# Scores of 256 queries in one go in five PSUM banks, with q and k turned in fp32 ahead of their split: thresholded attention and a MoE layer on one core

## The chip, the cores and the metric

The kernel runs on one core of one Trainium2 chip. The metric is device time in microseconds (us) from the first to the last instruction of the program; the median of three runs before the change is 545.32 us. Engines are called as in the profile: PE is TensorE (PEld its weight loads), DVE is VectorE, ACT is ScalarE, POOL is GpSimd, and SP is SyncE, which here issues most DMAs.

## What is computed

```python
# batch 8, heads 8, seq 576, head_dim 64; tau 0.02
scores = q @ k.T / sqrt(64)                        # per batch and head, 576 x 576
scores = where(scores >= max(scores) - tau, scores, -1e9)
attn   = exp(scores - max(scores)); attn /= sum(attn) + 1e-9
x      = (attn @ v), heads side by side            # 4608 tokens x 512
out    = leaky_relu(x @ w_in, 0.01) @ w_out        # 512 -> 2048 -> 512
```

q, k, v, the weights and the output are fp32 in DRAM. The threshold lies only 0.02 below the maximum, so the scores must be near fp32: q and k are each multiplied by 64 and split into two fp16 halves (high and low), and three products (high x high, low x high, high x low) are summed in PSUM.

## The kernel before

Each batch has 576 queries: two blocks of 256 and a tail of 64. Heads go in pairs; the first head of a pair has rows 0 to 63 of every turned tile, the second rows 64 to 127. A **step** is 128 queries of a head pair (`c` is the half of the 256-query block): `scores` (L195) runs twelve matmuls of 288 columns into two PSUM tiles of two banks each, which are double buffered; `copy_min` (L213) scales and copies them to SBUF on DVE with a running minimum (the scores are negated); `threshold` (L222) adds tau on POOL; `exps` (L226) and `weights` (L254) make the thresholded weights, on ACT and DVE, or, for one of the two heads of a "steep" step, on ACT alone (L242 and L243). After two steps, `recip` (L260) on DVE and `widen` (L264) on POOL put the reciprocal sums beside the weights, and `turn_w` (L268) has SP issue a transposing DMA of the weights. Four steps later `pv` (L273) multiplies by v, and `evacuate` (L287) scales the result into `x` on DVE. There are 18 steps in a batch, 144 in all: 64 of the pairs are full ones, 16 steps are tails of two head pairs each.

When four pairs of a block have their `x`, sixteen MoE units are queued: `layer1` (L315) multiplies by w_in into PSUM tile `hp` and applies the leaky ReLU on ACT (`g`), `layer2` (L331) accumulates `g` times w_out into PSUM tile `o`, which ACT copies to `osb`; `store` (L346) writes it out. In each step one `layer1` and two `layer2` calls are issued.

q and k of the next batch are loaded by SP (L73, L82), multiplied by 64 and split on POOL (L128, L139, L144) into fp16 halves, and each half is turned by PE (`turn`, L160: eight fp16 transposes for a unit, which is one head pair of q or k) into a PSUM tile that shares the tag "h" and its two buffers with `hp`; ACT copies the turned halves to `qT` and `kT` (L181). PSUM's eight banks go to scores (4), "h" (2), `pv` (1) and `o` (1).

The schedule is manual: every engine works in the order in which the loop at L454 issues, and each instruction waits on semaphores. The tables `loads_at`, `turns_at` and `pool_at` say in which step loads, turns and splits are issued. SP's queue holds the loads, the transposing DMAs and the stores, in the order of issue.

Of the kernel before, what the change touches and what calls it, by code (L numbers as in the profile page):

```python
# [14 lines left out]
PV_LAG = 4  # L15
# [12 lines left out]
class Step:  # L28


    def __init__(self, n, b, blk, p, c):
        self.n, self.b, self.blk, self.p, self.c = n, b, blk, p, c
        self.tail = blk == 2
# [3 lines left out]
def kernel(  # L37
# [24 lines left out]
    ident = sb.tile([128, 128], FP16, name="ident")  # L62
    minus_tau = sb.tile([128, 1], FP32, name="minus_tau")


# [3 lines left out]

    raws, tails, vraws, vtails = {}, {}, {}, {}  # L70
    SRC = {"q": q, "k": k}

    def load_main(b, s, which, eng=None, parts=1):  # L73
        t = sb.tile([128, 4, 256], FP32, tag="raw", bufs=4, name="raw")
        n = 4 // parts
        for i in range(parts):
            (eng or nc.sync).dma_start(
                out=t[:, ds(n * i, n), :],
                in_=SRC[which][b, ds(4 * s + n * i, n), 0:MAIN, :].rearrange("h (p t) d -> p h (t d)", t=4))
        raws[b, s, which] = t  # L80

    def load_tails(b, which, eng=None):  # L82
        t = sb.tile([128, 2, 2, 64], FP32, tag="rawt", bufs=2, name="rawt")
        src = SRC[which][b, :, MAIN:S, :].rearrange("(u sh) p d -> u p sh d", u=2)
        for u in range(2):
            (eng or nc.sync).dma_start(out=t[ds(64 * u, 64), :, :, :].rearrange("p s h d -> p (s h) d"), in_=src[u])
        tails[b, which] = t
# [23 lines left out]

    WIDE = {"q": 576, "k": 640}
    turned, halves, scaled = {}, {}, {}
# [6 lines left out]
    def pair_of(b, p, which):  # L122
        return raws[b, p // 2, which][:, ds(2 * (p % 2), 2), :].rearrange("p h (t d) -> p h t d", d=64)

    def new_half():
        return sb.tile([128, 2, 4, 2, 64], FP16, tag="half", bufs=4, name="half")

    def split_scale(key):  # L128
        t = sb.tile([128, 4, 2, 64], FP32, tag="scaled", bufs=2, name="scaled")
        if key[1] == "t":  # L130
            src = tails[key[0], key[2]][:, :, :, :]
            dst = t[:, 0:2, :, :]
        else:
            src = pair_of(*key)
            dst = t[:, :, :, :].rearrange("p t h d -> p h t d")
        nc.gpsimd.tensor_scalar(out=dst, in0=src, scalar1=64.0, scalar2=1.0, op0=AX.mult, op1=AX.mult)  # L136
        scaled[key] = t

    def split_high(key):  # L139
        n = 2 if key[1] == "t" else 4  # L140
        halves[key] = new_half()
        nc.gpsimd.tensor_copy(out=halves[key][:, 0, 0:n, :, :], in_=scaled[key][:, 0:n, :, :])  # L142

    def split_low(key):  # L144
        n = 2 if key[1] == "t" else 4
        nc.gpsimd.tensor_tensor(out=halves[key][:, 1, 0:n, :, :], in0=scaled.pop(key)[:, 0:n, :, :],  # L146
                                in1=halves[key][:, 0, 0:n, :, :], op=AX.subtract)

    def split_now(key):
        t = halves[key] = new_half()  # L150
        for i in range(2):
            if key[1] == "t":
                src, n = tails[key[0], key[2]][:, :, i, :], 2
            else:
                src, n = pair_of(*key)[:, i, :, :], 4
            nc.scalar.activation(out=t[:, 0, 0:n, i, :], in_=src, func=AF.Copy, bias=0.0, scale=64.0)  # L156
            nc.vector.scalar_tensor_tensor(out=t[:, 1, 0:n, i, :], in0=src, scalar=64.0, in1=t[:, 0, 0:n, i, :],
                                           op0=AX.mult, op1=AX.subtract)

    def turn(key, copy=None):  # L160
        copy = copy or nc.scalar.copy
        b, p, which = key
        dst, half = turned_of(b, which), halves.pop(key)
        n = 2 if p == "t" else 4
        c0 = 0 if which == "q" else 64
        if p == "t":
            c0 = MAIN if which == "q" else 0
            tp = ps.tile([128, 2, 2, 2, 64], FP16, tag="h", bufs=2, name="tp")
        else:
            tp = ps.tile([128, 2, 4, 128], FP16, tag="h", bufs=2, name="tp")  # L170
        for x in range(2):
            for t in range(n):
                o = tp[:, x, :, t, :] if p == "t" else tp[:, x, t, :]
                nc.tensor.transpose(o, half[:, x, t, :, :].rearrange("p h d -> p (h d)"), ident[:, :])  # L174
        if p == "t":
            for x in range(2):
                copy(out=dst[:, x, :, ds(c0, 64)], in_=tp[:, x, :, :, :].rearrange("d u s p -> d (u s) p"))
            if which == "k":
                nc.gpsimd.tensor_copy(out=dst[:, :, :, 576:640], in_=dst[:, :, :, 0:64])
        else:  # L180
            copy(out=dst[:, :, p, ds(c0, 512)], in_=tp[:, :, :, :].rearrange("d x t p -> d x (t p)"))  # L181

    steps = []
    for b in range(B):
        for blk in range(2):
            for p in range(NP):
                for c in range(2):
                    steps.append(Step(len(steps), b, blk, p, c))  # L190
        for c in range(2):
            steps.append(Step(len(steps), b, 2, 2 * c, c))
    PERB = len(steps) // B

    def scores(st):  # L195
        st.sc = [ps.tile([128, 2, 512], FP32, tag="sc", bufs=2, name=f"sc{h}") for h in range(2)]
        for kh in range(2):
            for i, (qx, kx) in enumerate(((0, 0), (1, 0), (0, 1))):
                for u in range(2 if st.tail else 1):
                    for h in range(2):  # L200
                        pair = st.p + u
                        rows = ds(64 * h, 64)
                        key0 = 64 * (1 - h) + 288 * kh
                        if st.tail:
                            lhs = turned[st.b, "q"][rows, qx, pair, MAIN:S]
                            o = st.sc[h][ds(64 * u, 64), kh, 0:288]
                        else:
                            lhs = turned[st.b, "q"][rows, qx, pair, ds(256 * st.blk + 128 * st.c, 128)]
                            o = st.sc[h][:, kh, 0:288]
                        nc.tensor.matmul(out=o, lhsT=lhs, rhs=turned[st.b, "k"][rows, kx, pair, ds(key0, 288)],  # L210
                                         start=(i == 0), stop=(i == 2), skip_group_check=True)

    def copy_min(st):  # L213

        st.mn = sb.tile([128, 2], FP32, tag="mn", bufs=3, name="mn")
        st.s = sb.tile([128, 2, 576], FP32, tag="s", bufs=2, name="s")
        for h in range(2):
            nc.vector.tensor_scalar(  # L218
                out=st.s[:, h, :].rearrange("p (a b) -> p a b", a=2), in0=st.sc[h][:, :, 0:288],
                scalar1=-1.0 / UNIT, scalar2=None, op0=AX.mult, op1=AX.min, accum_out=st.mn[:, h : h + 1])  # L220

    def threshold(st):  # L222
        st.th = sb.tile([128, 2], FP32, tag="th", bufs=3, name="th")
        nc.gpsimd.tensor_scalar(out=st.th[:, :], in0=st.mn[:, :], scalar1=1.0, scalar2=tau_f, op0=AX.mult, op1=AX.add)  # L224

    def exps(st):  # L226

        c = 0 if st.tail else st.c
        if c == 0:
            pairs["now"] = pr = Pair()  # L230
            pr.w = sb.tile([128, 2, 10, 128], FP16, tag="w", bufs=3, name="w")
            pr.sum = sb.tile([128, 2, 2], FP32, tag="sum", bufs=3, name="sum")
            pr.n = 1 if st.tail else 2
        st.pair = pr = pairs["now"]
        flat = pr.w[:, c, :, :].rearrange("q n d -> q (n d)")
        st.w = [flat[:, ds(576 * h, 576)] for h in range(2)]
        st.sum = [pr.sum[:, c, h : h + 1] for h in range(2)]
        st.e = sb.tile([128, 2, 576], FP16, tag="e", bufs=2, name="e")
        for h in range(2):
            if h and st.steep:  # L240
                z = st.s[:, h, :]
                nc.scalar.activation(out=z, in_=z, func=AF.Prelu, bias=st.th[:, h : h + 1], scale=-1.0, alpha=1e20)  # L242
                nc.scalar.activation(out=st.w[h], in_=z, func=AF.Exp, bias=minus_tau[:, :], scale=1.0,  # L243
                                     accum_out=st.sum[h])
            else:
                nc.scalar.activation(out=st.e[:, h, :], in_=st.s[:, h, :], func=AF.Exp, bias=st.mn[:, h : h + 1],  # L246
                                     scale=-1.0)

    pairs = {}

    class Pair:
        pass
# [267 lines left out]
```

## Time and profile before

| | |
|---|---|
| runs, us | 541.51, 545.32, 548.29; median 545.32 |
| profiled execution: span, us | 545.5 |
| its mean granted TensorE clock | 0.967 |
| first and last score matmul, us from the start | 8.1 and 503.3 |
| first layer 1 matmul | 63.1 |
| last weights on DVE | 508.0 |
| full transposing DMAs on SP: number, median time of the issue | 68, 3.25 us |
| DMA moved | 90.04 MB, 165 GB/s |

The span is the profiled execution's own time, from its first to its last instruction. Busy time counts an engine's instructions and not its waits; idle time ahead of a group is put down to the instruction that ended it. For SP the rows are issues: a DMA's row ends when its descriptors are handed over, and landing comes later (5.2 us in the median from issue to landing for the transposing DMAs). The chain of waits is followed back from the last instruction.

### The profile page before, as it was taken

To read this page: it belongs to the slowest core of one execution; us is meant where nothing else is said; L and a number is where in the kernel's file an instruction comes from. 1 tells how busy PE (TensorE), PEld (TensorE's weight loads), DVE (VectorE), ACT (ScalarE), POOL (GpSimd) and SP (SyncE) were. 2 spreads that over 40 slices of the span, in tenths; PEclk is the share of its full clock that TensorE was granted. 3 is DMA by queue.
4 is the path that set the end of the run, shared out by engine and by line. 5 is a ranking of instruction groups with operands and counts; after the bars stand their busy time and mean duration, and the time that the engine had idled before them with its cause. 6 is when DMAs were issued, how large, how long until landed. Compare 5 with 4: busy or idle time off the path is not lost.

```text
span 545.5 us, 14102 instructions
## 1 busy us (share of the span) xinstructions
PE 495.6 (91%) x5312; PEld 315.6 (58%) x5312; DVE 422.5 (77%) x1163; ACT 428.2 (79%) x726; POOL 319.8 (59%) x562
## 2 busy tenths in 40 slices
PE   4557656799999999999999999999999999999996
PEld 2334434565665666666666666666666666656672
DVE  3458555889899998899889988999889988788200
ACT  3678645687888888898889888898888888999541
POOL 5777553967676667767676767666676764112000
PEclk9987678899999999999999999999999999999999
DMA  9868999557997789698978899798988876767601
GB/s 211 226 162 151 200 155 170 119 116 154 216 211 143 169 196 193 166 193 154 219 150 190 150 210 195 163 192 185 203 164 169 169 171 144 144 110 136 136 40 58
DMA packets 231044, 90.04 MB, mean 165 GB/s; under 512 B 201280, under 2 KB 227904, under 8 KB 230976
## 3 DMA queue, kind: packets, MB, share of 16 engines
q1 hardware_dynamic: 227744, 84.43, 76.2%
q0 software_dynamic: 2688, 4.19, 5.1%
q8 instruction: 41, 0.67, 0.5%
q10 hardware_dynamic: 544, 0.52, 0.3%
q14 instruction: 27, 0.22, 0.1%
HBM read 36.70 MB, written 9.44 MB: 85 GB/s over the span
## 4 chain that ended last, share of the span: by engine, by line
PE 70%; DVE 10%; DMA 8%; POOL 4%; issue 4%; ACT 3%; SPq 0%; POOLq 0%; DVEq 0%
PE hp L324 21%; PE o L336 20%; PE sc L210 18%; PE pv L282 8%; DMA wT<-w 6%; DVE s L218 5%; DVE w L256 4%; PE tp L174 4%; DMA raw<-in_k_dram 2%; POOL half L142 1%; POOL scaled L136 1%; POOL half L146 1%; ACT w L243 1%; DVE x L304 1%; ACT s L242 1%
## 5 line engine op out<-in xcount | busy, mean ns | idle before, releaser
L218 DVE TENSOR_SCALAR_CACHE_REDUCE s<-sc 128x576 f32<-128x576 f32 x288 | 204.8, 749 | 70.3 <-PE sc L210 62.8
L256 DVE SCALAR_TENSOR_TENSOR w<-s,th,e 128x576 f16<-128x576 f32 x210 | 190.7, 930 | 2.4 <-POOL th L224 1.7
L210 PE MATMUL sc<-kT,qT 64*128 64x288 f16 (+1 forms) x1920 | 146.4, 299 | 17.8 <-DVE s L218 10.2
L246 ACT ACTIVATE e<-s,mn 128x576 f16<-128x576 f32 x210 | 155.8, 774 | 5.1 <-DVE s L218 5.1
L336 PE MATMUL o<-wout,g 128*128 128x512 f16 x576 | 146.8, 379 | 0.7 <-ACT osb L342 0.7
L324 PE MATMUL hp<-x,win 128*128 128x256 f16 x1024 | 136.7, 277 | 0.2 <-ACT g L326 0.2
L324 PEld LDWEIGHTS <-win 128*128 128x128 f16 x1280 | 106.1, 99 | 44.3 <-issue 31.9
L210 PEld LDWEIGHTS <-qT 64*128 64x128 f16 (+1 forms) x1920 | 81.2, 100 | 77.2 <-issue 52.3
L265 POOL CAST w<-rec 128x256 f16<-128x256 f32 (+1 forms) x80 | 30.1, 376 | 149.5 <-DVE rec L262 138.5
L326 ACT ACTIVATE g<-hp 128x512 f16<-128x512 f32 x144 | 84.2, 585 | 40.0 <-PE hp L324 39.1
L242 ACT ACTIVATE s<-s,th 128x576 f32<-128x576 f32 x78 | 60.4, 774 | 53.9 <-POOL th L224 53.6
L146 POOL TENSOR_TENSOR half<-scaled,half 128x512 f16<-128x512 f32 (+1 forms) x77 | 83.0, 1079 | 6.0
L336 PEld LDWEIGHTS <-g 128*128 128x128 f16 x576 | 53.4, 98 | 38.3 <-issue 1.2
L282 PE MATMUL pv<-wT,v 128*64 128x256 f16 (+1 forms) x960 | 57.4, 257 | 19.9 <-DMA wT<-w 14.5
L282 PEld LDWEIGHTS <-v 128*64 128x64 f16 x960 | 37.4, 112 | 52.9 <-issue 23.8
L142 POOL CAST half<-scaled 128x512 f16<-128x512 f32 (+1 forms) x77 | 61.9, 804 | 4.9
L243 ACT ACTIVATE w<-s,minus_tau 128x576 f16<-128x576 f32 x78 | 60.5, 775 | 2.5
L174 PE MATMUL tp<-ident,half 128*128 128x128 f16 x576 | 49.0, 231 | 6.6 <-ACT half L156 5.0
L136 POOL TENSOR_SCALAR scaled<-raw 128x512 f32<-128x512 f32 x62 | 49.4, 796 | 4.8 <-DMA raw<-in_k_dram 1.4
L224 POOL TENSOR_SCALAR th<-mn 128x2 f32<-128x2 f32 x144 | 40.8, 283 | 17.1 <-DVE s L218 4.5
L174 PEld LDWEIGHTS <-half 128*128 128x128 f16 x576 | 40.7, 104 | 12.1 <-ACT half L156 5.0
L181 ACT COPY kT<-tp 128x1024 f16<-128x1024 f16 x32 | 32.1, 1004 | 0.0
(32 smaller groups left out, 245.2 us busy)
## 6 DMA issues: line engine op xcount, KB each, us to landing
vraw<-in_v_dram SPq DMA_DIRECT2D x16, 512.0 KB, 5.1
out_dram<-osb SPq DMA_DIRECT2D x16, 512.0 KB, 3.4
raw<-in_k_dram SPq DMA_DIRECT2D x14, 512.0 KB, 4.3
raw<-in_q_dram SPq DMA_DIRECT2D x14, 512.0 KB, 4.7
win<-in_moe_w_in_dram POOLq DMA_DIRECT2D x4, 512.0 KB, 9.9
wout<-in_moe_w_out_dram POOLq DMA_DIRECT2D x4, 512.0 KB, 12.1
wT<-w SPq DMA_TRANSPOSE x80, 5.2
raw<-in_k_dram SPq DMA_DIRECT2D x4, 256.0 KB, 10.6
```

The costliest lines, as they stand in the source:

```text
L142: nc.gpsimd.tensor_copy(out=halves[key][:, 0, 0:n, :, :], in_=scaled[key][:, 0:n, :, :])
L146: nc.gpsimd.tensor_tensor(out=halves[key][:, 1, 0:n, :, :], in0=scaled.pop(key)[:, 0:n, :, :], in1=halves[key][:, 0, 0:n, :, :], op=AX.sub ...
L174: nc.tensor.transpose(o, half[:, x, t, :, :].rearrange("p h d -> p (h d)"), ident[:, :])
L210: nc.tensor.matmul(out=o, lhsT=lhs, rhs=turned[st.b, "k"][rows, kx, pair, ds(key0, 288)], start=(i == 0), stop=(i == 2), skip_group_check= ...
L218: nc.vector.tensor_scalar(out=st.s[:, h, :].rearrange("p (a b) -> p a b", a=2), in0=st.sc[h][:, :, 0:288], scalar1=-1.0 / UNIT, scalar2=No ...
L243: nc.scalar.activation(out=st.w[h], in_=z, func=AF.Exp, bias=minus_tau[:, :], scale=1.0, accum_out=st.sum[h])
L246: nc.scalar.activation(out=st.e[:, h, :], in_=st.s[:, h, :], func=AF.Exp, bias=st.mn[:, h : h + 1], scale=-1.0)
L256: nc.vector.scalar_tensor_tensor(out=st.w[h], in0=st.s[:, h, :], scalar=st.th[:, h : h + 1], in1=st.e[:, h, :], op0=AX.is_le, op1=AX.mult, ...
L282: nc.tensor.matmul(out=o, lhsT=v16[st.b % 2][:, st.p + u, blk, :], rhs=rhs, start=(i == 0), stop=(i == 4), skip_group_check=True)
L324: nc.tensor.matmul(out=hp[:, jj, :], lhsT=w_in16[:, i, ts(j, 128)], rhs=g.x[:, i, :], start=(i == 0), stop=(i == 3), skip_group_check=True)
L326: nc.scalar.activation(out=g.g[:, ds(nj * u, nj), :], in_=hp[:, :, :], func=AF.Prelu, bias=0.0, scale=1.0, alpha=0.01)
L336: nc.tensor.matmul(out=g.o[:, :], lhsT=g.g[:, j, ts(m, 128)], rhs=w_out16[:, j, :], start=(j == 0), stop=(j == 15), skip_group_check=True)
```

## The change

The loop's unit becomes a **period**: 256 queries of a head pair (four score tiles of 128 x 576), or the tails of all four pairs; 9 in a batch, 72 in all. Each period issues two rounds of MoE (a round is one `layer1` and two `layer2`), so as many rounds per query as before. The scores of a period lie in one PSUM tile of five banks, `sc`, which is not double buffered. The four tiles of 576 columns stand side by side and cross bank borders, so each is computed in two pieces; pieces of both heads share bank 2, and a dependency is added by hand that keeps the second head's piece there (`b12`) behind the first head's (`a12`). It goes over SP: a `nop` on SP waits for the matmul of `a12`, and the matmul of `b12` waits for the `nop`.

The threshold of a period becomes one DVE instruction for its four tiles, three tiles go the plain way (exp on ACT, weights on DVE) and one the steep way (ACT alone), always. One transposing DMA per period takes the weights out; pv follows two periods later, and its PSUM tile moves to tag "h". q and k are turned in fp32: POOL multiplies and reorders a unit (`bring`), PE turns it with four fp32 transposes, ACT takes it out as fp32 (`take_out`), and POOL then splits it into the halves (`split`). The three units turned ahead of the loop are split by ACT and DVE straight from PSUM, and batch 0 is loaded head by head with the order of elements that the turn needs, so it isn't brought.

Order of issue in period n: loads and stores (SP), scores, four copies and threshold, turns and take-outs, POOL's splits and brings, then exp, MoE round, two exps, MoE round, steep pair, pv of period n-2, two weights, `x` of period n-2, the third weights, reciprocal, widening and transpose.

```diff
-PV_LAG = 4
+PV_LAG = 2
...
+    sc = ps.tile([128, 2560], FP32, name="sc")
+    PLACE = {(0, 0): 128, (1, 0): 704, (0, 1): 1856, (1, 1): 1280}
...
+    def scores(st):
+        (a00, a01), (b01, b00) = pieces(0, 0), pieces(0, 1)
+        (a11, a12), (b12, b11) = pieces(1, 0), pieces(1, 1)
+        todo = [[(1, a12), (0, a00), (0, a01), (1, a11)], [(0, b00), (0, b01), (1, b11), (1, b12)]]
...
+            for mm in product(st, c, h, x, i):
+                if (h, x) == (1, b12) and i == 0:
+                    tc.add_manual_dep(mm.ins, signal.ins.name, BEHIND, reason="the row halves share a bank")
+                last = mm
+            if (h, x) == (0, a12) and i == 2:
+                signal = nc.sync.nop()
+                tc.add_manual_dep(signal.ins, last.ins.name, BEHIND, reason="the row halves share a bank")
...
+    def copies(st):
...
+        for n, t in enumerate(TILES):
+            st.s[t] = sb.tile([128, 576], FP32, tag=f"s{n}", bufs=1, name="s")
+            nc.vector.tensor_scalar(out=st.s[t][:, :], in0=sc[:, ds(PLACE[t], 576)], scalar1=-1.0 / UNIT, scalar2=None,
+                                    op0=AX.mult, op1=AX.min, accum_out=st.mn[:, n : n + 1])
+        nc.vector.tensor_scalar(out=st.th[:, :], in0=st.mn[:, :], scalar1=1.0, scalar2=tau_f, op0=AX.mult, op1=AX.add)
...
+    def finish(st):
+        rec = sb.tile([128, 2, 2], FP32, tag="rec", bufs=2, name="rec")
+        nc.vector.reciprocal(out=rec[:, :, :], in_=st.sum[:, :, :])
+        nc.gpsimd.tensor_copy(out=st.w[:, :, 9, :].rearrange("q c (h d) -> q c h d", h=2),
+                              in_=rec[:, :, :].unsqueeze(3).to_broadcast([128, 2, 2, 64]))
+        st.wt = sb.tile([128, 2, 10, 128], FP16, tag="wT", bufs=4, name="wT")
+        nc.sync.dma_start_transpose(out=st.wt[:, :, :, :].rearrange("k c n q -> k (c n) q"),
+                                    in_=st.w[:, :, :, :].rearrange("q c n d -> q (c n d)"))
...
-        st.pv = ps.tile([128, 4, 128], FP32, tag="pv", bufs=1, name="pv")
+        st.pv = ps.tile([128, 2, 128], FP32, tag="h", bufs=2, name="pv")
...
+            tp = ps.tile([128, 4, 128], FP32, tag="h", bufs=2, name="tp")
+            src = ready.pop(key)
+            for t in range(4):
+                nc.tensor.transpose(tp[:, t, :], src[:, t, :, :].rearrange("p h d -> p (h d)"), ident[:, :])
...
+        for h in range(2):
+            eng.dma_start(out=t[:, :, h, :], in_=SRC[which][0, 2 * p + h, 0:MAIN, :].rearrange("(p t) d -> p t d", t=4))
...
+        while stores:
+            store()
+        st = periods[n] if n < N else None
+        if st:
+            scores(st)
+            copies(st)
+        for key in turns_at.get(n, []):
+            turn(key)
+            take_out(key)
```

## The prediction

> **What bounds the kernel now.** I read the page first: busy shares, then the slices of clock, then the chain that ended last.
>
> ```profile
> PE 495.6 (91%) x5312; PEld 315.6 (58%) x5312; DVE 422.5 (77%) x1163; ACT 428.2 (79%) x726; POOL 319.8 (59%) x562
> PEclk9987678899999999999999999999999999999999
> PE 70%; DVE 10%; DMA 8%; POOL 4%; issue 4%; ACT 3%; SPq 0%; POOLq 0%; DVEq 0%
> PE hp L324 21%; PE o L336 20%; PE sc L210 18%; PE pv L282 8%; DMA wT<-w 6%; DVE s L218 5%; DVE w L256 4%; PE tp L174 4%; DMA raw<-in_k_dram 2%; POOL half L142 1%; POOL scaled L136 1%; POOL half L146 1%; ACT w L243 1%; DVE x L304 1%; ACT s L242 1%
> ```
>
> The reader is to see that TensorE is the bound from about 110 us on, and that SP (SPq) has no share: nothing on the chain waits for SP's queue. Next I read the grouped rows for the price of one instruction, and the timeline for pitches and for SP.
>
> ```profile
> L218 DVE TENSOR_SCALAR_CACHE_REDUCE s<-sc 128x576 f32<-128x576 f32 x288 | 204.8, 749 | 70.3 <-PE sc L210 62.8 <-ACT g L326 1.7 <-ACT osb L342 1.4
> L265 POOL CAST w<-rec 128x256 f16<-128x256 f32 x64 | 25.5, 398 | 125.9 <-DVE rec L262 115.0 <-POOL v L110 5.7 <-issue 4.2
> L262 DVE RECIPROCAL rec<-sum 128x4 f32<-128x4 f32 x64 | 11.4, 178 | 5.5 <-ACT w L243 0.9
> ```
>
> ```profile
> 297.31 3.01 SPq L270 DMA_TRANSPOSE wT<-w  x1
> ...
> 300.38 0.58 SPq L77 DMA_DIRECT2D raw<-in_q_dram  x1
> ...
> 302.90 0.18 DVE L262 RECIPROCAL rec<-sum 128x4 f32<-128x4 f32 x1
> ...
> 303.14 0.40 POOL L265 CAST w<-rec 128x256 f16<-128x256 f32 x1 [1.27 <-DVE rec L262]
> 303.57 3.88 SPq L270 DMA_TRANSPOSE wT<-w  x1
> ```
>
> Two things to see: the transpose starts 0.03 us after the widening that it needs (303.54), so its row holds no wait for it; and SP's next instruction (300.38) starts only when the transpose's 3.01 us are over. Issuing one transpose holds SP's queue for 3 to 4 us (68 full ones: median 3.25). Last, the clock beside TensorE's work:
>
> ```profile
> 72.05:75.46 3.41, 0.00 (x0) 0.00 (x0) 2.51 (x6) 1.62 (x3) 3.35 (x5) 1.00 1.33 181
> 75.46:78.87 3.41, 1.42 (x14) 0.91 (x18) 0.00 (x0) 1.65 (x3) 2.98 (x6) 0.50 1.45 145
> 78.87:82.29 3.42, 3.42 (x36) 1.95 (x32) 1.94 (x6) 0.12 (x1) 0.16 (x1) 0.50 1.09 101
> 82.29:89.11 6.82, 2.21 (x40) 1.68 (x32) 4.16 (x12) 4.63 (x7) 5.06 (x9) 1.00 1.34 129
> ```
>
> Columns: window, PE, PEld, DVE, ACT, POOL busy, granted clock, DMA. A window of 3.41 us with an idle PE is followed by half clock, until a window full of work has passed.
>
> **The change, part by part.** Pitches (start to next start, medians of the steady timeline): score block of 12 matmuls 0.84, of layer 1 0.88, of layer 2 (four matmuls) 0.96, pv 0.67, eight fp16 transposes 0.45; copy 0.68, weights 0.74 to 0.81, plain exp 0.67, Prelu of `hp` 0.48, the steep pair 0.80 + 0.87. The steady pace now: scores start at 8.1 and end at 503.3 us, 72 pairs of steps, about 6.84 us each, of which PE has 2 x (0.84 + 0.88 + 0.96) + 0.67 + 1.11 x 0.45 = 6.5.
>
> What the change lightens: take-outs of 512 fp32 values (as `g` from `hp`, pitch 0.48) for copies of 1004 ns, 64 of them, some 25 us of ACT; 144 thresholds (283 ns, 40.8 us) leave POOL for 72 small DVE instructions, 0.15 each by the reciprocal of the same shape; 80 transposing DMAs become 72. None of this is on PE, so alone it is worth little. Summed per period, DVE would have 5.9, ACT 5.4 us. Matmul columns of scores, layers and pv are unchanged.
>
> PE's fp32 transposes: four per unit instead of eight. No row shows an fp32 transpose. Lower end 56 ns each as fp16, 0.22 a unit; upper end four times that, 0.90 (1.11 units a period). I take the lower; the upper adds 0.55 to a period in the loop below. The Trainium skill ("FP8 and Floating Point Precision", TensorE Precision Notes) says that true fp32 takes four passes through the array; by it the sum would stand at the upper end. No run here shows it yet.
>
> The new wait. In each period the first of the last three matmuls of head 1 (`b12`) waits for a signal that SP passes on (`nc.sync.nop`). SP works in order, and what stands ahead of signal n in its queue is: the transpose of period n-1, which waits for POOL's widening, which waits for the reciprocal that ends DVE's work on period n-1; then the loads and stores of period n. Behind `b12` on PE stand the turns, both rounds of layers 1 and 2, and pv of period n. And `sc` is one tile, so the first copy of period n waits for the last score matmul. DVE issues the copies of period n after the reciprocal of n-1, and pv, exp and weights of period n come before the reciprocal of n. So the wait closes a ring over SP that is passed once per period. Its length from reciprocal to reciprocal, at full clock, in us:
>
> - Reciprocal's end to widening 0.07, widening 0.40, to SP 0.03, issue of the transpose 3.25: 3.74. Two of the 68 issues took over 8 us, early in the run; I take the median, and 3.05 and 3.53 (the mean) as ends.
> - SP's loads and stores: 15.5 of them in nine periods at 0.58 to 0.70 with 0.04 between: 1.12 a period. Signal at 4.94.
> - SP to PE, bounded by 0.03 to 0.1 like other handoffs, 0.07; weights 0.1, three matmuls of 256 columns 0.32, drain 0.17: copies start at 5.63 and end, with the read of the last minimum, at 8.42; threshold done 8.65.
> - PE goes on at 5.43: turn to 5.66, first `hp` 6.64, second 8.5, pv ready 10.1.
> - ACT in order: take-out 5.9, exp 6.5, Prelu 7.2, two exps from 7.65, Prelu 9.0, half an `osb` 0.24, steep pair 9.7 to 11.4.
> - DVE: weights 8.65 and 9.4, `x` 10.2, third weights 10.55 to 11.4, reciprocal done 11.6.
>
> A period of 11.6 us against 6.84, and TensorE stands idle for about 5.2 of it (scores up to `b12` of the next period are done by 11.4, the signal comes at 4.94 of the next). By the rows on the clock, an idle stretch of 5.2 us leaves at least one 3.41 us window mostly empty, so the work after the signal starts at half clock, for 2.6 to 5.8 us depending on where the windows fall. Every microsecond at half clock puts the second `hp` and pv half a microsecond later, and both are on the way to the reciprocal: 1.3 to 2.9 us more, 12.9 to 14.5. A period longer than four windows moves the next window's boundary nearer to the signal, and the half-clock stretch shrinks with it; a shorter one does the opposite. So the period is drawn to four windows, 4 x 3.413 = 13.65 us. I take this value; the upper price of fp32 transposes changes the stretch, not the four windows.
>
> Start and end. SP's first loads become 20 issues for 16, in runs of 256 bytes, and each beyond the eighth waits for an earlier landing; now SP is through at 19.5 us, I take 22 (19 to 27) for the first signal and 5.3 from copies to reciprocal: 28. Five periods without MoE at 11.2 (10.9 at full clock): 56. 66 periods x 13.65 = 901. After the last reciprocal eleven iterations of MoE remain, 32.5 on PE, and 5 until the store has landed; 38, as now 37.5 from the last weights (508.0) to the end. Sum: 28 + 56 + 901 + 38 = 1023 us. The profiled span, 545.5, agrees with the median of the runs, 545.32, so nothing is added.
>
> Edits at nothing: POOL's split (0.8 + 1.1 a unit, plus 0.8 to bring) lies in the long period beside the ring; without that cover it would delay the widening, which stands behind it on POOL. pv in the `h` buffers: its third user; the buffer it takes was freed by a Prelu a microsecond earlier.
>
> **The rivals.**
> 1. The ring as above, with the clock kept (a partly busy window need not count as idle: 82.29 to 89.11 kept full clock over two windows with 2.21 us of work, the second of them empty): 28 + 5 x 10.9 + 66 x 11.6 + 38 = 886. The upper fp32 price makes it 922.
> 2. Other side: the signal does not wait behind the transpose. Then PE's own 6.0 + 0.6 per period decides: 10.6 + 72 x 6.6 + 38 = 524, faster by 4%. Against it stands every SP row: the next instruction never starts within a transpose's span. It decides only if the signal comes within 0.2 us of the reciprocal, since without the relay the ring is 6.7.
> 3. SP's share is short. The Trainium skill ("DMA: Bandwidth & Descriptors", Issuing engines are not separate DMA queues) says that the time to initiate a DMA on a sequencer is usually small relative to the DMA itself. As a mechanism of this kernel: the transpose is issued like a load, 0.58 for 3.25, the ring is 8.95, and the time 28 + 5 x 8.3 + 66 x 8.95 + 38 = 698. The rows say 3.0 to 3.9 of 5.2 us to landing.
>
> **How the numbers follow.** The ring with half clock 0.57, with full clock 0.30, short issue 0.04, no ring 0.09. About 2% is what a measurement of this kernel tells from no change. Only the last case holds faster (0.05) and same (0.04); slower has 0.91. The predicted time is that of the first case, 1023 us. Its own ends: 12.9 to 15 us a period, 973 to 1112; the second case's lower end, with an issue of 3.05, is 873. The range 870 to 1110 takes in both and leaves out some 2 in 10.
>
> **What would show it.** Right: in the profile after, PE's weight loads of scores or SPq among the waits, with idle PE of over 4 us in every period; SPq rows of the transpose followed at once by the signal, then by the last score matmuls, then by four copies in a row; DVE's idle time ahead of the copies some 5 us x 72; granted clock of 7 in the steady slices, against 9 for rival 1; DMA_TRANSPOSE still about 3.2 on SP. The fp32 transposes' pitch settles their price. Wrong: a period under 8 us, or a PE busy above 80% at full clock, would mean that the signal is not held up by the transpose.

## The result, and the profile after

The changed kernel takes 1045.69 us (median of four runs, 1043.32 to 1047.84), the kernel before 546.4 beside it (541.51 to 548.29): 1.916 times as long, 95% interval 1.905 to 1.926. It is slower by far more than a measurement can miss. The profiled execution has a span of 1044.5 us at a mean granted clock of 0.776. (Runs of the kernel before scatter from 536 to 553 us over all that follows, and the ratios are made from undisturbed runs alone, so a ratio is not always the quotient of the two medians beside it.)

The page of the changed kernel: busy time, PE's and the clock's slices, the chain, and four groups with the idle time ahead of them.

```profile
PE 641.1 (61%) x5024; PEld 403.3 (39%) x5024; DVE 477.1 (46%) x1227; ACT 404.0 (39%) x693; POOL 252.3 (24%) x389
PE   1443446656566766565666655666656656666687
PEclk9996677777787777777777767777677777777799
...
issue 10%; PE 2%; DMA 1%; POOL 1%; ACT 0%; POOLq 0%
...
L222 PE MATMUL sc<-kT,qT 64*128 64x192 f16 (+7 forms) x1920 | 165.4, 324 | 384.3 <-SPq L241 371.8
...
L252 DVE TENSOR_SCALAR_CACHE_REDUCE s<-sc 128x576 f32<-128x576 f32 x288 | 201.0, 754 | 407.2 <-PE sc L222 407.2
...
L284 POOL CAST w<-rec 128x256 f16<-128x256 f32 x72 | 28.6, 398 | 317.8 <-DVE rec L283 293.0
```

PE was busy for 91% of the span and is now for 61%, at a clock of 7 tenths, and no other engine comes near to full. The copies cost what they did (754 ns against 749), but DVE idles for 407 us ahead of them, where it idled for 70 in all. PE in turn idles for 372 us ahead of the score matmuls, released by `SPq L241`, which is the signal. POOL idles for 293 us until the reciprocal. Each waits for the next: a ring. The chain that ended last accounts for 14% of the span only, so it can't be read as a whole; the view of the waits is used instead. Its columns are the wait, its total in us, how often, and the longest:

```profile
DVE s L252 <- PE sc L222: 407.2, 72, 11.4
PEld L222 <- SPq L241: 392.7, 72, 10.3
PE sc L222 <- SPq L241: 371.8, 72, 10.0
ACT scaled L178 <- PE tp L150: 328.4, 61, 12.9
POOL w L284 <- DVE rec L283: 293.0, 63, 12.6
```

The wait for the signal is there 72 times, once in each period, with 5.2 us each. The timeline of the changed kernel shows one turn of the ring (start, duration, instruction, and in brackets how long its engine had waited and for what):

```profile
505.14 0.18 DVE L283 RECIPROCAL rec<-sum 128x4 f32<-128x4 f32 x1 [0.33 <-ACT w L272]
...
505.39 0.40 POOL L284 CAST w<-rec 128x256 f16<-128x256 f32 x1 [5.14 <-DVE rec L283]
505.81 3.06 SPq L287 DMA_TRANSPOSE wT<-w  x1
508.92 0.58 SPq L72 DMA_DIRECT2D raw<-in_k_dram  x1
...
509.61 0.85 PE L222 MATMUL sc<-kT,qT 64*64 64x256 f16 x10 [4.68 <-SPq L241]
...
510.50 0.76 DVE L252 TENSOR_SCALAR_CACHE_REDUCE s<-sc 128x576 f32<-128x576 f32 x1 [5.18 <-PE sc L222]
...
518.49 0.18 DVE L283 RECIPROCAL rec<-sum 128x4 f32<-128x4 f32 x1
```

The reciprocal ends at 505.32, the widening at 505.79, the transpose has been issued at 508.87, a load at 509.50, and only then do the last score matmuls start (509.61), then the copies (510.50), and 8 us later the next reciprocal. The windows of the same kernel (window, PE, PEld, DVE, ACT, POOL busy, granted clock, DMA share, GB/s) give the clock of the steady stretch:

```profile
84.00:980.00 896.00, 557.15 (x4382) 350.67 (x4383) 426.85 (x1104) 354.31 (x610) 222.83 (x337) 0.74 0.38 84
```

PE is busy for 62% of that time, at a granted clock of 0.74. The first reciprocal ends at 34.4 us, the last at 1007.4. The same view around the turn of the ring above shows how this mean comes about:

```profile
501.24:508.07 6.83, 3.69 (x60) 2.42 (x57) 2.16 (x6) 3.78 (x7) 0.40 (x1) 1.00 0.17 33
508.07:514.90 6.83, 5.29 (x27) 3.07 (x28) 4.26 (x12) 2.97 (x5) 2.93 (x6) 0.50 0.63 144
```

PE idles for 4.68 us up to 509.61, from 508.07 the granted clock is 0.50, and it stays there for 5.3 us after the signal. In the steady stretch the clock has these two values alone, mostly for 6.83 us each in turn.

For all kernels with the relay on SP and the transpose ahead of it, the ring can be split at the same events. Means in us over the last 63 periods (all but the first batch), worked out from the traces:

| kernel | to widening | widening, to SP | transpose's issue | to signal | signal to first copy | first copy to reciprocal | period | granted clock |
|---|---|---|---|---|---|---|---|---|
| changed | 0.07 | 0.43 | 3.05 | 0.99 | 0.90 | 8.21 | 13.65 | 0.75 |
| `e3_warm` | 0.08 | 0.43 | 3.17 | 1.03 | 0.61 | 6.89 | 12.19 | 0.96 |
| `e6_loads_behind` | 0.07 | 0.42 | 3.05 | 0.06 | 0.88 | 8.12 | 12.61 | 0.78 |
| `e7_extra_issue` | 0.07 | 0.42 | 3.06 | 1.57 | 0.89 | 8.07 | 14.09 | 0.75 |

### The profile page after: what moved, and what is told of

It reads as the page before. It is cut to its first block, busy times and chain, and to the rows that moved or that the text cites. A ratio compares the mean times of both kernels' runs of the same rounds, so it can differ in the third digit from the quotient of the medians.

```text
span 1044.5 us, 13454 instructions
## 1 busy us (share of the span) xinstructions
PE 641.1 (61%) x5024; PEld 403.3 (39%) x5024; DVE 477.1 (46%) x1227; ACT 404.0 (39%) x693; POOL 252.3 (24%) x389
## 5 line engine op out<-in xcount | busy, mean ns | idle before, releaser
L222 PE MATMUL sc<-kT,qT 64*128 64x192 f16 (+7 forms) x1920 | 165.4, 324 | 384.3 <-SPq L241 371.8
L222 PEld LDWEIGHTS <-qT 64*128 64x128 f16 (+1 forms) x1920 | 97.5, 104 | 433.0 <-SPq L241 392.7
L178 ACT ACTIVATE scaled<-tp 128x512 f32<-128x512 f32 (+1 forms) x77 | 42.6, 555 | 414.6 <-PE tp L150 328.4
L338 PE MATMUL hp<-x,win 128*128 128x256 f16 x1024 | 191.9, 351 | 0.4 <-ACT scaled L178 0.3
L350 PE MATMUL o<-wout,g 128*128 128x512 f16 x576 | 190.3, 466 | 0.7 <-ACT osb L356 0.7
L338 PEld LDWEIGHTS <-win 128*128 128x128 f16 x1280 | 149.5, 125 | 73.3 <-issue 31.7
L284 POOL CAST w<-rec 128x256 f16<-128x256 f32 x72 | 28.6, 398 | 317.8 <-DVE rec L283 293.0
L150 PE MATMUL tp<-ident,ready 128*128 128x128 f32 x224 | 58.4, 428 | 0.0
L134 POOL TENSOR_SCALAR ready<-raw 128x512 f32<-128x512 f32 x56 | 42.2, 759 | 43.4 <-DMA raw<-in_q_dram 36.0
L319 DVE TENSOR_TENSOR x<-pv,wT 128x256 f16<-128x256 f32 x64 | 27.1, 423 | 49.0 <-PE pv L299 48.9
L184 POOL TENSOR_TENSOR qT<-scaled,qT 128x512 f16<-128x512 f32 (+1 forms) x39 | 48.0, 1230 | 3.2
```

Source lines behind the costliest of these rows:

```text
L150: nc.tensor.transpose(tp[:, t, :], src[:, t, :, :].rearrange("p h d -> p (h d)"), ident[:, :])
L184: nc.gpsimd.tensor_tensor(out=half_of(key, 1), in0=t, in1=half_of(key, 0), op=AX.subtract)
L222: yield nc.tensor.matmul(out=o, lhsT=lhs, rhs=turned[st.b, "k"][rows, kx, pair, ds(key0, n)], start=(i == 0), stop=(i == 2), skip_group_ch ...
L338: nc.tensor.matmul(out=hp[:, jj, :], lhsT=w_in16[:, i, ts(j, 128)], rhs=g.x[:, i, :], start=(i == 0), stop=(i == 3), skip_group_check=True)
L350: nc.tensor.matmul(out=g.o[:, :], lhsT=g.g[:, j, ts(m, 128)], rhs=w_out16[:, j, :], start=(j == 0), stop=(j == 15), skip_group_check=True)
```

## The experiments

The theory is the ring over SP with a clock that falls because TensorE waits in it. The rivals are those of the prediction: that some other part of the change is the cost (the single score tile, the fp32 transposes, the order of the MoE rounds), that the clock adds nothing, or that the period sticks to four clock windows.

**The relay over another engine** (`e1_relay_act`). SP no longer stands between the two matmuls:

```diff
-                signal = nc.sync.nop()
+                signal = nc.scalar.nop()
```

> The changed kernel with one edit: the relay that keeps one score piece behind the other goes over ACT's queue instead of SP's. Ring theory: the transposing DMA (3.06 us) and SP's loads (1.1 us) leave the ring, the period falls from 13.65 to PE's own work, 6.5 to 7.2 us, the granted clock is back at 1.0 in the steady part, and the time is 530 to 600 us. Rival (the single score tile without double buffering, the fp32 transposes or the bunched MoE rounds are what costs): still over 800 us.

Measured: 563.18 us (561.64 to 567.19), 1.038 times the kernel before (1.023 to 1.053). One moved instruction takes back 482 of the 499 us. All else of the change was left in, and it costs 4% (2 to 5) in this form. The steady period is 6.82 us in the mean, 6.41 in the median; once in a batch one lasts 8.8 to 12.4. (In the kernel before, the same 63 periods take 6.56 us each; the 6.84 of the prediction is a mean over the whole run, the slow start included.) Two of the waits from 150 to 500 us point to the reason:

```profile
POOL ready L134 <- DMA raw<-in_q_dram: 28.5, 7, 6.1
PEld tp L150 <- POOL ready L134: 15.0, 5, 3.7
```

The loads of q are still behind the transposes in SP's queue and come late, so POOL can't bring the unit and PE can't turn it.

**The transposes behind the signal** (`e2_t_behind_signal`). The relay stays on SP; instead the transpose of period n-1 is issued after the scores of n, so that it stands behind signal n in the queue. `finish` keeps the reciprocal and the widening, and `turn_w` has the DMA:

```diff
         if st:
             scores(st)
+        if 1 <= n <= N:
+            turn_w(periods[n - 1])
+        if st:
             copies(st)
```

> The changed kernel with one edit: the transposing DMA of period n-1 is issued on SP behind the signal of period n, instead of ahead of it. Everything else stays, the relay over SP too. Ring theory: the signal no longer waits for the reciprocal of the period before, the ring opens, 530 to 600 us, as with the relay over ACT. If a relay over SP costs in itself (any hop over that engine), it stays over 700 us.

Measured: 559.59 us (557.66 to 561.17), 1.029 times the kernel before (1.019 to 1.040). A relay on SP costs little as long as the transpose of the period just before isn't ahead of it (that of one period earlier still is). The windows of this kernel:

```profile
150.00:500.00 350.00, 334.03 (x3659) 234.47 (x3659) 323.99 (x899) 282.01 (x500) 164.99 (x262) 1.00 0.82 170
```

PE is busy for 95% of the stretch at a clock of 1.00, and a period takes 6.63 us against 6.56 in the kernel before. Waits for the signal have shrunk to this, in the same stretch:

```profile
PEld L222 <- SPq L241: 15.6, 12, 2.0
```

The last reciprocal ends 10.5 us later than in the kernel before, and 5.9 of these are lost in the first batch. The first signal comes at 24.7 us, behind SP's first loads, where DVE began its first copy at 10.6 us before; between 60 and 100 us issues of 5.9 to 8.2 us, beside the loads of the weights, hold the signal up twice, by 4.3 and 4.4 us.

**TensorE kept busy while it waits** (`e3_warm`). Ahead of `b12`, 64 idle matmuls of 128 columns write to unused columns of `sc`; nothing reads them, and the rest is the changed kernel:

```diff
+            if (h, x) == (1, b12) and i == 0:
+                for _ in range(64):
+                    nc.tensor.matmul(out=sc[:, 0:128], lhsT=w_in16[:, 0, 0:128], rhs=w_in16[:, 0, 128:256], ...)
```

> The changed kernel with 64 idle matmuls of 128 columns (about 3.5 us at full clock, results not used) on PE in each period, just ahead of the matmul that waits for SP's signal. They fill part of the wait of 5 to 6 us and lengthen nothing else. Theory: the ring at full clock is 11.6 to 12.2 us, and half clock adds the rest to 13.65; with PE kept busy the granted clock goes to 1.0 and the time to 860 to 940 us. Rival: the clock follows from the wait and costs nothing on the ring, then 1045 us or more.

Measured: 953.74 us (950.91 to 956.58), 1.755 times the kernel before (1.721 to 1.788). TensorE has more to do, and the kernel is 92 us faster than the changed one. The page and the timeline of this kernel:

```profile
PEclk9778789998999999999999979999999999999999
```

```profile
504.73 3.75 PE L238 MATMUL sc<-win 128*128 128x128 f16 x64
...
508.98 0.50 PE L222 MATMUL sc<-kT,qT 64*128 64x256 f16 x5 [0.50 <-SPq L245]
```

The wait at the signal is down to 0.50 us in this row (over the run PE waits 124.8 us for it in place of 371.8), and the five score matmuls behind it take 0.50 us. In the changed kernel such a row reads:

```profile
524.37 0.82 PE L222 MATMUL sc<-kT,qT 64*128 64x256 f16 x5 [5.92 <-SPq L241]
```

The table says what the clock is worth: 0.29 us from the signal to the copies, 1.32 from there to the reciprocal, 1.6 in a period of 13.65. The period is only 1.46 shorter, since the issue of the transpose is 0.12 longer here. The ring itself stays, at 12.19. The time came out within 14 us of the upper end of what was expected, since the full-clock ring is longer than the prediction's 11.6.

**The relay alone, in the kernel before** (`e4_before_relay`). The scores of each step get one wait on a signal over SP, and nothing else of the change (`i` counts the three products, `kh` the halves of the keys, `u` the head pairs of a tail):

```diff
+                        if (kh, i, u, h) == (0, 2, 0, 0):
+                            signal = nc.sync.nop()
+                            tc.add_manual_dep(signal.ins, mm.ins.name, BEHIND, reason="relay")
+                        if (kh, i, u, h) == (1, 2, 0, 1):
+                            tc.add_manual_dep(mm.ins, signal.ins.name, BEHIND, reason="relay")
```

> The kernel before with the relay alone: in each step one of the last score matmuls waits for a signal that SP passes on after an earlier matmul. Scores stay double buffered, transposes stay fp16. The signal stands behind the transposing DMA of the pair before in every second step. Ring theory: transpose 3.1, loads 0.6 to 1.1, scores 0.5, copies 1.4, exp and steep pair to the reciprocal 2 to 3, widening 0.5, so 8 to 9.5 us a pair against 6.84: 640 to 760 us. Rival (the relay is harmless where scores are double buffered): 540 to 560 us.

Measured: 987.26 us (986.92 to 987.59), 1.816 times the kernel before (1.784 to 1.848). The direction was expected, the size not at all. The page's clock and the waits of this kernel:

```profile
PEclk9976777777777778778777778777877777877799
```

```profile
PEld L212 <- SPq L215: 334.6, 73, 9.9
DVE s L225 <- PE sc L212: 522.9, 146, 9.0
```

It is the same picture, 4.6 us in each of 73 waits and a clock of 7 tenths. A pair of steps takes 13.1 us in the mean, so double-buffered scores do not save it: the relay alone, without the rest of the change, costs 440 of the 499 us. In the full pairs the signal comes 4.1 us after the reciprocal of the pair before, and from there to the next reciprocal it takes 9.2 us. The expectation had about 4 to 5 for that second part and so counted too little of a pair's work on PE, ACT and DVE; this part was not split further.

**Both at once** (`e5_both`): the edits of `e1_relay_act` and `e2_t_behind_signal` together.

> The changed kernel with the relay over ACT and, besides, the transposing DMA of period n-1 issued on SP behind the scores and loads of period n, so that loads of q and k no longer wait behind a transpose. Ring theory: nothing of the ring is left, steady periods of about 6.6 us as in the run with the transpose behind the signal (6.63 against 6.84 for a pair of steps in the kernel before), and the first reciprocal at 28 instead of 33 us: 540 to 555 us, the same as the kernel before. If the rest of the change (bunched MoE rounds, one score tile, fp32 turns) costs by itself in the steady part, 560 us or more.

Measured: 530.24 us (529.70 to 533.39, six runs) against 547.34 of the kernel before (eleven runs): 0.987, interval 0.981 to 0.992. The time is below the 540 to 555 us expected. This is the one version faster than both kernels: its slowest run lies below the fastest of the kernel before, 536.21. Its page:

```profile
PE 478.7 (91%) x5024; PEld 335.8 (64%) x5024; DVE 448.6 (85%) x1227; ACT 393.9 (75%) x693; POOL 250.9 (47%) x389
```

TensorE bounds it again. Its busy time fell by 16.9 us, from 495.6, and the profiled span by as much (528.6 against 545.5). Periods take 6.40 us in the mean (6.15 in the median) against 6.56 before. So the rest of the change, with the transposes issued later, is a small gain. Whether the change or the new order on SP brings it is open: no run has that order in the kernel before.

**Loads behind the signal** (`e6_loads_behind`) **and one more issue ahead of it** (`e7_extra_issue`). Two sizes of the same stretch of the ring, to tell whether the period is drawn to four windows of the clock. In the first the block of loads and stores moves from the loop's head to behind the copies. In the second SP issues one unused load of 32 KB ahead of each signal:

```diff
+                nc.sync.dma_start(out=junk[:, :], in_=moe_w_in[0:128, 0:64])
                 signal = nc.sync.nop()
```

> The changed kernel with one edit: the loads and stores of period n are issued on SP behind the signal of period n instead of ahead of it. They are 1.1 us a period of SP's time on the ring. If the period is drawn to four clock windows of 3.41 us (13.65), the shorter ring is made up for by a longer stretch at half clock: 1005 to 1045 us. If the lengths simply add, 72 x 1.1 = 80 us come off: about 965 us.

> The changed kernel with one more small load (32 KB, not used) issued on SP ahead of each signal, about 0.65 us of SP's time on the ring in each of 72 periods. If the period is drawn to four clock windows: 1045 to 1065 us. If the lengths simply add: 1045 + 72 x 0.65 = 1092 us.

Measured: 972.64 us (971.75 to 976.03), 1.808 (1.798 to 1.819), and 1078.13 us (1075.30 to 1081.09), 2.002 (1.987 to 2.018). The first is near the plain sum, 965. The second lies between the two expectations, 1065 at most and 1092. A stretch of 0.93 us taken out of the ring shortens the period by 1.04, from 13.65 to 12.61; 0.58 put in lengthens it by 0.44, to 14.09. The waits for the signal of the two kernels, of the first and of the second:

```profile
PEld L222 <- SPq L241: 325.6, 72, 9.7
```

```profile
PEld L223 <- SPq L243: 438.4, 72, 11.1
```

Against the changed kernel's 392.7 that is 67 less and 46 more, 0.93 and 0.63 in a period: what SP issues ahead of the signal is what PE waits. The period follows the sum in the main and is not held at four windows. The changed kernel's own trace says so too: single periods after the first batch last 11.5 to 16.8 us, and the means of the seven batches run from 12.4 to 14.05. A weak pull remains in the second kernel: the half clock lasts 4.3 us beyond the signal there, against 4.9 in the changed kernel, and the stretch from the first copy on is 0.14 shorter. In the first kernel, where the half clock should have lasted longer, it is 4.3 as well.

## Why the prediction was right, and where it was not

- **The ring over SP: right.** Waits, timeline, `e1_relay_act` and `e2_t_behind_signal` agree. The rival in which the signal isn't behind the transpose (524 us) and the one with a short issue (698) are both out: the issue holds SP for 3.05 us in the ring, 0.2 below the value taken. By the Trainium skill ("DMA: Bandwidth & Descriptors", Issuing engines are not separate DMA queues) the time to initiate a DMA is usually small relative to the DMA itself. Here it is 3.05 us of the 4.9 us from issue to landing (the last number of the row from the changed kernel's page below), and the measurement decides.

```profile
wT<-w SPq DMA_TRANSPOSE x72, 4.9
```

- **The clock: right in kind and within its bounds.** Keeping PE busy gave 1.6 us back in each period, where 1.3 to 2.9 was said; the half clock lasts 4.9 us beyond the signal in the mean, where 2.6 to 5.8 was said. The rival with full clock (886) is out: `e3_warm` shows what such a ring takes, and the changed kernel isn't there.
- **The step that failed is the last of the period: "So the period is drawn to four windows".** `e6_loads_behind` and the batches of the changed kernel show a sum of terms, and `e7_extra_issue` does for three quarters of what it puts in. The steady mean is 13.65 us all the same, by chance: reciprocal to transpose's end 3.55 (said 3.74), loads and signal 0.99 (1.20), signal to copies 0.90 (0.69 at full clock), copies to reciprocal 8.21 (5.97 at full clock). The sum of terms without that step, 12.9 to 14.5, holds it.
- **The term that was mis-sized is copies to reciprocal.** At nearly full clock, in `e3_warm`, it is 6.89 and not 5.97. The difference builds up on DVE: the first weights start 3.31 us after the first copy's start (said 3.02), the second 4.26 (3.77), `x` 5.35 (4.57), the third weights 5.68 (4.92). The wait for pv is only 0.14 of this in the mean. The weights were taken at a pitch of 0.74 to 0.81, which goes with a duration of 0.81, but the mean duration in the kernel before is 0.93 (930 ns in its row):

```profile
L256 DVE SCALAR_TENSOR_TENSOR w<-s,th,e 128x576 f16<-128x576 f32 x210 | 190.7, 930 | 2.4 <-POOL th L224 1.7
```

In `e3_warm` one takes 0.81 us where POOL runs nothing beside it (118 of 216) and 944 ns over all. In the changed kernel `x` starts at 6.63. The 1.28 between the two, nearly all that the clock costs in this term, is 0.68 more waiting for pv, 0.41 more for an exp on ACT, and a threshold that takes 0.19 longer.

- **fp32 transposes: between the bounds.** At full clock four of them take 0.49 us (302.50 to 302.99 below, in `e5_both`, from the first of a unit to the next layer 1; the median of 31 units is the same), so 123 ns each, where eight in fp16 took 0.45.

```profile
302.50 0.66 PE L150 MATMUL tp<-ident,ready 128*128 128x128 f32 x4
302.99 1.06 PE L340 MATMUL hp<-xt,win 128*128 128x128 f16 x16
```

The lower bound, 0.22, was taken. By the rule of the Trainium skill that the prediction cites ("FP8 and Floating Point Precision", TensorE Precision Notes), true fp32 takes four passes. At four times the fp16 price a unit would be 0.90; this run shows 2.2 times, and the measurement decides.

- **The threshold on DVE: 0.556 us in the mean, and 0.15 was said.** See the last section.
- **Start and end.** The first reciprocal is at 34.4 us (said 28), the first signal at 26.1 (said 22); the five light periods take 65.8 (said 56); the other 66 take 907.2, or 13.75 each (said 901); the rest 37.1 (said 38). The errors, 6.4 + 9.8 + 6.2 - 0.9, are the 21.5 us between 1023 and the span of 1044.5. Three quarters of it lie ahead of the MoE, where the time from the first signal to the first reciprocal was 8.3 us, near the 9.1 of a steady period, and not 6.

The single score tile shows no loss of its own: in `e2_t_behind_signal` and `e5_both` it is still there, and their steady periods are 6.63 and 6.40 us against 6.56 before.

## What to carry to other kernels

A semaphore that is passed on by a queue with slow instructions in it costs what is ahead of it in that queue; before a dependency is relayed, write down what stands there, what that waits for in turn, and whether it leads back to the waiter. If it does, the period is close to the sum around the ring, every engine in it idles, and TensorE pays twice: here its granted clock fell from 0.967 to 0.776 on top of its waits. When a large change is slower, open the one new wait first: here 97% of the loss was in it, and with the transposes moved as well the kernel was 1.3% faster than before.

## What the runs showed of the hardware that was not expected

The threshold instruction, 128 x 4 values on DVE, has a price that depends on what POOL does. Two rows of it in the changed kernel's timeline, the first with the POOL instruction that runs beside it:

```profile
499.08 1.16 POOL L184 TENSOR_TENSOR qT<-scaled,qT 128x512 f16<-128x512 f32 x1
...
499.46 0.81 DVE L254 TENSOR_SCALAR th<-mn 128x4 f32<-128x4 f32 x1
...
513.33 0.17 DVE L254 TENSOR_SCALAR th<-mn 128x4 f32<-128x4 f32 x1
```

In 43 of 72 periods POOL runs its subtract (`TENSOR_TENSOR`) when the threshold starts: it then takes 0.81 us in the mean and ends 0.02 to 0.03 us after the subtract, every time. In the 13 where POOL runs nothing it is 0.17; in the other 16 POOL runs something else, and it takes 0.17 to 0.47 and again ends after POOL's instruction. The weights behave alike: 0.81 us in 135 cases where POOL runs nothing beside them, up to 1.70 beside its subtract. The copies of the scores don't: 0.75 in the mean either way. That the two engines get into each other's way is read from this alone; no run took it apart.

In `e3_warm` 64 matmuls that nobody reads made the kernel 9% faster (953.74 against 1045.69): in a ring that contains TensorE, the clock during its wait is part of the price.
